# Clustered attention with a spectral gate on one core: routing turned by VectorE, alternating score banks, another last inverse, dummy matmuls in front

## The chip, the cores and the metric

One core of a Trainium2 chip. The metric is the time of one execution on the device in microseconds; the kernel before takes 423.12 us (median of three runs, 422.86 to 423.76). TensorE (PE in the profile) multiplies matrices into PSUM, which has eight banks of 512 fp32 a partition here; VectorE (DVE), ScalarE (ACT) and GpSimd (POOL) work on tiles; SyncE (SP) only issues DMAs. Each engine runs its own instruction stream in order.

## The reference, cut to what matters

```python
# q, k, v: (4, 8, 768, 64); centroids: (8, 16, 64)
q_assign = argmax(einsum('bhsd,hcd->bhsc', q_n, c_n), -1)   # q_n, k_n, c_n: rows scaled to length 1
k_assign = argmax(einsum('bhsd,hcd->bhsc', k_n, c_n), -1)
mask = q_assign[:, :, :, None] == k_assign[:, :, None, :]
scores = where(mask, scale * q @ k^T, -1e9)
attn = softmax(scores) @ v
x = attn with the heads side by side                         # (4, 768, 512)
x1, x2, x3 = split(x @ w_proj, 3)
x2_conv = irfft(rfft(x2) * rfft(filter_fft))                 # over the 768 positions
out = (x1 * x2_conv * x3) @ w_out
```

## The kernel before

**A planner writes the order.** The body calls `op(engine, duration, function, reads, writes, due, ...)` for each small piece of work. `Plan.run` (line 175) then simulates the engines with these durations and emits the pieces in the order of that simulation: of the pieces that are ready it takes, for each engine, the one with the lowest score, which is its due time plus `WAIT` times the wait until it could start, less `SAME` where TensorE stays in the same array mode (line 212). A due time is lowered to what the successors need (line 180). Where a piece names two engines, the one that would end first gets it. `step(i)` (line 375) is the due time of attention step `i`; `SPANS` (line 27) gives those of the four hyenas. The result is a fixed program; the chip only follows it.

**Attention.** The 32 heads go in 16 pairs, two heads on the two halves of the partitions. For each pair:

- `load_pair` (line 389) loads q, k and v from HBM on SP's queue; loads of later pairs stand behind the masks of pair 0 (`masks0`).
- `routing` (line 593) turns q and k by fp32 transposes on TensorE (line 606), copies them to `qkT`, casts them on GpSimd into the operands `aug` (line 613), multiplies by the normed centroids into 4 x 32 rows of a bank, one strip of 32 rows for each of q and k and each half of the sequence (line 623, `sim`), copies that to SBUF (line 626), turns it on TensorE with three fp32 transposes so that the 16 clusters lie along the free axis (line 631), finds the first maximum with five VectorE operations (lines 636 to 642), turns the one-hot back with six bf16 transposes on TensorE into 64 rows by 768 (line 650), scales and shifts it by `mk` on its way out of PSUM (lines 655 and 657: q's rows become 0 or -262144, k's rows 0 or 1), and puts it into 16 extra rows of `aug` with four small DMAs (line 664). With those rows in the operands, a score of two different clusters comes out far below zero.
- `attend` (line 673), six times: scores of 128 keys against 768 queries of both heads into three banks (line 685), one exponential over 1536 columns into `pb` (line 689), its product with v accumulated in two banks (line 699), and a running sum of `pb` on VectorE (line 709).
- `finish` (line 715): sums over the keys, their reciprocals by way of DRAM, the scaled result `rb`, the sum and difference of its halves `uT`, and a bf16 copy `xT`.

**PSUM.** `BankPool.choices` (line 92) says which banks a piece may take: scores always banks 0 to 2, the attention output 3 and 4, all else 5 to 7, and more where attention hasn't begun or no scores are left.

**Hyena.** After each four pairs (one batch), `hyena` (line 775) does the projections, the transform as products with sine and cosine tables `fw`, the product with the filter's spectrum (lines 804 and 807), the inverse transform with `inv`, and the output product. The inverse of a block of 128 channels (line 844) splits into an even part `pe` and an odd part `po`; ScalarE or VectorE copies `po` to `od` (line 858), VectorE forms sum and difference `yy` (line 860), and line 863 multiplies by `x13`, the product of the two gates.

**In front.** `constants`, `centroid` (norms of the centroids), `angles` (line 454: 15 VectorE operations, then six sine activations on ScalarE with a table of their own, line 496), `inverse_tables` (line 508: `inv` by transposing `fw`) and `filter_tables` (line 536: the filter's spectrum, scaled on VectorE into `hm`) prepare tables while pairs 0 and 1 begin.

## Time and profile before

| | |
|---|---|
| median of the runs | 423.12 us |
| the profiled execution: its time, its span | 422.92 us, 421.1 us |
| first and last scores' exponential begin | 21.87 us, 343.51 us |
| last attention product begins | 347.16 us |
| mean granted TensorE clock | 0.984 |
| SP's queue: raw loads, masks, stores | 64, 62, 24 issues |

The span runs from the first to the last instruction. A row of the timeline gives the start in us, the duration in us, engine, line, operation, output and input tiles, how many instructions were merged, and in brackets how long the engine had been idle and what released it. A row of the groups gives the number of instructions, total busy us, mean ns, and the idle time ahead of them. Matmuls overlap in a pipeline, so the distance from start to start says more than a duration. In a table of stretches each engine's busy us is followed by its count of instructions, and then come the granted clock of TensorE, the share of the DMA engines and GB/s.

### The profile page before, as it was taken

How to read it: one execution, taken by the hardware profiler on the slowest of the kernel's cores; microseconds unless marked ns; L12 is line 12 of the kernel's file. 1: busy time of each engine (PE TensorE's matmuls, PEld its weight loads, DVE VectorE, ACT ScalarE, POOL GpSimd, SP SyncE). 2: the span in 40 equal slices, each digit the busy share in tenths (PEclk: the TensorE clock that was granted, in tenths of full speed). 3: DMA queues.
4: the chain of work that ended last, by engine and by line, in shares of the span. 5: the costliest groups of instructions: out<-in, count | busy, mean ns of one | idle time of the engine just before them, and what ended most of it. 6: DMA issues, size and time to landing. Idle time of an engine off the chain costs nothing. (4 is left out here: it accounts for less than half of the span.)

```text
span 421.1 us, 8711 instructions
## 1 busy us (share of the span) xinstructions
PE 393.9 (94%) x3485; PEld 213.6 (51%) x3485; DVE 354.4 (84%) x414; ACT 256.5 (61%) x317; POOL 120.9 (29%) x114
## 2 busy tenths in 40 slices
PE   4489998999999999999999999999999999998794
PEld 2245444445445565655454545545655467555442
DVE  5959977898989898989879799999899788947673
ACT  2477655888577767555775766666676654344242
POOL 5722333155253140532405051407113002101000
PEclk9869999999999999999999999999999999999998
DMA  8199956544363314020365711110311002200123
GB/s 183 20 226 216 222 128 148 129 99 93 87 158 86 84 45 115 10 77 3 76 161 161 164 40 48 48 40 4 84 41 40 3 10 81 101 2 2 75 76 149
DMA packets 68943, 37.17 MB, mean 88 GB/s; under 512 B 56940, under 2 KB 62632, under 8 KB 68904
## 3 DMA queue, kind: packets, MB, share of 16 engines
q1 hardware_dynamic: 67640, 34.45, 31.9%
q0 software_dynamic: 1056, 2.10, 2.7%
q8 instruction: 27, 0.44, 0.4%
q10 hardware_dynamic: 208, 0.08, 0.1%
q14 instruction: 12, 0.10, 0.1%
HBM read 30.66 MB, written 6.48 MB: 88 GB/s over the span
## 5 line engine op out<-in xcount | busy, mean ns | idle before, releaser
L689 ACT ACTIVATE pb<-scores 128x1536 f32<-128x1536 f32 x96 | 139.4, 1452 | 52.2 <-PE scores L324 50.9
L699 PE MATMUL outs<-pb,vraw 128*64 128x512 f32 (+1 forms) x768 | 143.2, 492 | 0.2 <-ACT osb L719 0.2
L313 POOL CAST aug<-qkT 64x768 bf16<-64x768 f32 x64 | 85.1, 1329 | 160.6 <-PE scores L324 80.3
L709 DVE TENSOR_TENSOR acc<-acc,pb 128x1536 f32<-128x1536 f32 x64 | 118.1, 1845 | 9.5 <-ACT pb L689 9.1
L699 PEld LDWEIGHTS outs<-pb,vraw 128*64 128x64 f32 x768 | 54.4, 137 | 66.2 <-issue 59.7
L324 PE MATMUL scores<-aug,aug 128*64 128x512 bf16 (+3 forms) x768 | 81.8, 332 | 5.1 <-DMA aug<-ohT 2.8
L324 PEld LDWEIGHTS <-aug 80*64 80x64 bf16 (+1 forms) x768 | 42.1, 111 | 35.0 <-issue 15.5
L324 PEld LDWEIGHTS <-wpj 128*64 128x64 bf16 x512 | 32.3, 110 | 16.6 <-issue 5.6
L324 PE MATMUL bank<-xT,wpj 128*64 128x384 bf16 x384 | 38.5, 326 | 0.0
L709 DVE TENSOR_TENSOR acc<-pb,pb 128x1536 f32<-128x1536 f32 x16 | 31.8, 1987 | 4.7 <-ACT pb L689 4.7
L606 PE MATMUL bank<-ident,raw 128*128 128x128 f32 x183 | 30.5, 294 | 5.5 <-DMA raw<-in_q_dram 5.4
L324 PEld LDWEIGHTS <-k 128*64 128x64 bf16 (+1 forms) x448 | 21.7, 108 | 22.3 <-issue 11.4
L863 POOL TENSOR_TENSOR k<-yy,x 128x768 bf16<-128x768 f32 x7 | 16.1, 2302 | 58.6 <-DVE yy L860 54.1
L606 PEld LDWEIGHTS bank<-ident,raw 128*128 128x128 f32 x183 | 20.6, 147 | 20.1 <-issue 11.5
L311 ACT COPY qkT<-bank 128x384 f32<-128x384 f32 x47 | 21.8, 482 | 10.3 <-PE bank L606 10.2
L313 POOL CAST xT<-rb 128x768 bf16<-128x768 f32 x8 | 10.6, 1325 | 45.3 <-PE bank L324 20.1
L769 DVE TENSOR_TENSOR uT<-rb 128x384 bf16<-128x384 f32 x32 | 21.4, 680 | 0.1
L324 PE MATMUL bank<-wpj,uT 128*64 128x512 bf16 x160 | 20.6, 380 | 0.0
L804 DVE TENSOR_TENSOR tm<-bank,hm 128x1024 f32<-128x1024 f32 x16 | 19.4, 1219 | 0.8 <-PE bank L533 0.7
L719 ACT COPY osb<-outs 128x769 f32<-128x769 f32 x16 | 12.8, 801 | 8.9 <-PE outs L699 8.9
L764 DVE SCALAR_TENSOR_TENSOR rb<-osb,rb 128x768 f32<-128x768 f32 x16 | 17.8, 1114 | 0.0
L324 PEld LDWEIGHTS <-uT 128*64 128x64 bf16 x192 | 12.6, 109 | 8.6 <-issue 1.9
(161 smaller groups left out, 440.6 us busy)
## 6 DMA issues: line engine op xcount, KB each, us to landing
raw<-in_q_dram SPq DMA_DIRECT2D x32, 192.0 KB
raw<-in_k_dram SPq DMA_DIRECT2D x32, 192.0 KB
vraw<-in_v_dram SPq DMA_DIRECT2D x16, 384.0 KB
rb<-dr SPq DMA_DIRECT2D x30, 192.0 KB
out_dram<-os SPq DMA_DIRECT2D x21, 256.0 KB
k<-in_moe_filter_fft_dram SPq DMA_DIRECT2D x4, 384.0 KB
wpj<-in_moe_w_proj_dram POOLq DMA_DIRECT2D x1, 1536.0 KB, 14.3
aug<-ohT SPq DMA_DIRECT2D x62, 24.0 KB
```

What stands on the lines that cost most here:

```text
L311: nc.scalar.copy(o, i)
L313: eng[e].tensor_copy(o, i)
L324: nc.tensor.matmul(out[64 * c:64 * c + 64], lhsT[:, 64 * c:64 * c + 64], rhs, **k)
L606: nc.tensor.transpose(ps.t[:, ts(t, 128)], rv[:, 3 * ch + t], identp.t)
L689: op("ACT", 1.48, lambda e: nc.scalar.activation(pb.t[:, :, :S], sps.t.rearrange("p (a b) -> p a b", a=2), Act.Exp, scale=0.125), r=[sps], ...
L699: nc.tensor.matmul(o.t[64 * hp:64 * hp + 64, lo:hi], vv.t[:, hp, ts(sk, D)], pb.t[:, hp, lo:hi], start=(sk == 0), stop=(sk == NT - 1))
L709: nc.vector.tensor_tensor(acc.t, a, pb.t[:, :, :S], op=Alu.add)
L719: op("ACT", 0.82, lambda e: nc.scalar.copy(osb.t, o.t[:, :S + 1]), r=[o], w=[osb], due=step(i) + 5.0)
L764: op("DVE", 0.98, lambda e: V.scalar_tensor_tensor(rb.t, osb.t[:, :S], osb.t[:, S:S + 1], rb.t, op0=Alu.add, op1=Alu.mult), r=[osb, rb], w ...
L769: op("DVE", 0.55, lambda e, e_=e_, alu=alu: V.tensor_tensor(uT.t[:, e_], x3()[:, :, :64], x3()[:, :, 64:], op=alu), r=[rb], w=[(uT, e_)], ...
L804: op("DVE", 1.2, lambda e, i=i, cs=cs, ps=ps, tm=tms[cs]: V.tensor_tensor(tm.t, ps.t.unsqueeze(1).to_broadcast([128, 2, DM]), hm.t[:, i, c ...
L863: op(("DVE", "POOL"), (0.95, 1.8), lambda e, dt=dt, yt=yt, x13=x13: eng[e].tensor_tensor(y2v()[:, dt], yt().rearrange("p t c -> p (t c)"), ...
```

## The change

- **Routing.** `sim` is turned by a VectorE transpose of 32 x 32 blocks straight from PSUM; the one-hot goes back by a second such transpose, within SBUF. Both sets of TensorE transposes, the copy of `sim` and two bank takings go. `ohT` is 128 x 384 in place of 64 x 768, `mk` has 128 rows, the scaling works in place, and each of the four mask DMAs becomes two of half the size.
- **Banks.** For the first 24 steps (`TWICE`) scores may take banks 5 to 7 as well as 0 to 2, and other work may take 0 to 2; the three single banks become one tile.
- **Last inverse.** For batch 3 (`DIRECT`), each block's two output halves are full accumulations of six products; the second uses negated tables (`minus`, made on GpSimd). A VectorE product with `x13` follows each straight from PSUM. `od`, `yy` and the sum and difference go there.
- **Front.** `warm` adds 8 and 6 pairs of matmuls on the identity whose results nobody reads. Twelve operations of the angles and the two sums of the filter may go to GpSimd, the scalings of the filter to ScalarE.
- **Planner.** Each group of pieces gets an offset to its due time (`NUDGE`, some 500 numbers from -170 to 313), `SAME` goes from 1.08 to 1.777 and `WAIT` from 82.17 to 148.96. `ADDED` is empty, so its branch in `attend` isn't taken.

```diff
-SAME, WAIT, ANGLES = 1.08, 82.17, 0.99
+DIRECT = (3,)
+ADDED = ()
+TWICE = 24
+SAME, WAIT, ANGLES = 1.777, 148.96, 0.99
+NUDGE = {
+    "const": -26.79, "cent": -40.87, "l0.0": -65.51, "l0.1": -29.45, "v0": -3.48, "l1.0": -122.7,
...
+        o.due += NUDGE.get(o.tag, 0.0)
...
         if k == "S":
-            return [(0, 1, 2)]
+            return [(0, 1, 2)] + ([(5, 6, 7)] if b.scores_begun < b.twice else [])
...
-        if not b.scores_left:
+        if not b.scores_left or 0 < b.scores_begun < b.twice:
             ok += [0, 1, 2]
...
+    def warm(at, n, due):
+
+        P.tag = f"warm{at:.0f}"
+        for _ in range(n):
+            ps = Val(psE)
+
+            def f(e, ps=ps):
+                halves(ps.t, identb.t, identb.t.unsqueeze(1).to_broadcast([128, 4, 128]), start=True, stop=True)
+            op("PE", 0.43, f, r=[identb], w=[ps], due=due, after=at, mode="C64", kind="warm")
...
+            both = (("DVE", "POOL"), (0.36, 0.6))
+            op(*both, lambda e, m=m, n=n: eng[e].tensor_scalar(n(), kc(), st.t[:, m:m + 1], None, op0=Alu.mult),
+               r=[(na, "k"), st], w=[(na, m)], due=due, shared=True)
...
+        op("POOL", 2.0, lambda e: nc.gpsimd.tensor_scalar(
+            minus.t[:, :2], inv.t[:, 2:4], -1.0, None, op0=Alu.mult), r=[inv], w=[(minus, 0)], due=step(60), shared=True)
...
-        op("DVE", 1.76, lambda e: nc.vector.tensor_tensor(fu(), lo.t, hi.t, op=Alu.add),
+        op(("DVE", "POOL"), (1.76, 3.3), lambda e: eng[e].tensor_tensor(fu(), lo.t, hi.t, op=Alu.add),
...
+        both = (("ACT", "DVE"), (0.59, 0.68))
...
-        op(("ACT", "DVE"), (0.486, 0.55), lambda e: copy(e, sim.t, ps.t[:, :384]), r=[ps], w=[sim], due=due)
...
-                nc.tensor.transpose(sT.t[:, ts(t, 128)], sim.t[:, ts(t, 128)], identp.t)
-        op("PE", 0.33, f, r=[sim, identp], w=[sT], takes=[mx, cand], due=due, mode="A")
+        op("DVE", 0.56, lambda e: nc.vector.transpose(sim.t, ps.t[:, :384]), r=[ps], w=[sim], due=due, kind="T1")
...
-                nc.tensor.transpose(tp[:64, t * 128:(t + 1) * 128], ov[:, t % 3, t // 3], identb.t)
-        op("PE", 0.35, f, r=[oh, identb], w=[oT], takes=[ohT], due=due, mode="C64")
+        op("DVE", 0.55, lambda e: V.transpose(ohT.t, oh.t.rearrange("p n c -> p (n c)")), r=[oh], w=[ohT], due=due,
+           kind="T2")
...
-        op(("DVE", "ACT"), (0.68, 0.815), f, r=[oT, mk], w=[ohT], due=due)
+        op(("DVE", "ACT"), (0.22, 0.48), f, r=[mk, ohT], w=[ohT], due=due)
...
+                for ch in range(2):
+                    def f(e, j=j, hp=hp, ch=ch):
+                        r0 = 64 * ch + 32 * j + 16 * hp
+                        eng[e].dma_start(aug.t[hp][j][64 - 16 * hp:80 - 16 * hp, ts(ch, 384)], ohT.t[r0:r0 + 16])
...
+            if b in DIRECT:
+                for e_ in range(2):
+                    ps = Val(psF)
+
+                    def f(e, dt=dt, ps=ps, e_=e_):
+                        for n in range(6):
+                            w = minus.t[:, n - 2] if e_ and n > 1 else inv.t[:, n]
+                            halves(ps.t[:, :384], yv()[:, n // 2, n % 2, ts(dt, 128)], w, start=(n == 0), stop=(n == 5))
+                    op("PE", 0.98, f, r=[y, inv] + [minus] * e_, w=[ps], takes=[y2], due=due, mode="C64", kind="I")
+                    op("DVE", 0.55, lambda e, dt=dt, ps=ps, e_=e_, x13=x13: V.tensor_tensor(
+                        y2v()[:, dt].rearrange("p (t a c) -> p t a c", a=2, c=64)[:, :, e_],
+                        ps.t[:, :384].rearrange("p (t c) -> p t c", c=64),
+                        x13.t.rearrange("p a b -> p (a b)").rearrange("p (t a c) -> p t a c", a=2, c=64)[:, :, e_],
+                        op=Alu.mult), r=[ps, x13], w=[(y2, (dt, e_))], due=due + 1)
...
+    warm(0.0, 8, FIRST - 300.0)
     routing(0)
+    warm(14.0, 6, T0 - 4.0)
```

More of the change, by code (lines that the diff above doesn't have):

```diff
@@ L134 @@
     __slots__ = ("alts", "fn", "deps", "succ", "need", "due", "vals", "takes", "mode", "lag", "size",
-                 "end", "n", "shared", "ready", "kind", "after", "left", "table")
+                 "end", "n", "shared", "ready", "kind", "after", "left", "table", "tag")
 class Plan:
@@ L509, in inverse_tables @@
         for j in range(6):
+            P.tag = f"inv{j}"
             ps = Val(psF)
@@ L705, in attend @@
             acc, last = accs[p], pbs[i - 1]
+            P.tag = f"acc{p}"
             def f(e):
```

188 lines of the change are left out of this document (107 added, 81 removed), and 69 rows, old and new, of the table NUDGE.

## The prediction

> **What bounds the kernel now.** I read the shares of the page first, then the busy time of five stretches cut where the picture changes, then the timeline of both ends.
>
> ```profile
> span 421.1 us, 8711 instructions
> PE 393.9 (94%) x3485; PEld 213.6 (51%) x3485; DVE 354.4 (84%) x414; ACT 256.5 (61%) x317; POOL 120.9 (29%) x114
> ```
> ```profile
> core 0: us, PE busy (x) PEld busy (x) DVE busy (x) ACT busy (x) POOL busy (x), PEclk, DMA share, GB/s
> 0.00:17.00 17.00, 9.12 (x51) 5.28 (x51) 11.85 (x31) 5.60 (x11) 12.22 (x31) 1.00 0.54 118
> 17.00:32.10 15.10, 10.28 (x66) 5.83 (x65) 9.71 (x20) 10.63 (x13) 5.05 (x15) 0.66 0.84 176
> 32.10:348.60 316.50, 314.15 (x2738) 165.43 (x2738) 283.48 (x301) 212.30 (x240) 97.86 (x68) 1.00 0.36 88
> 348.60:380.00 31.40, 30.25 (x322) 19.50 (x319) 23.24 (x35) 13.58 (x25) 3.94 (x2) 1.00 0.14 52
> 380.00:421.10 41.10, 30.11 (x320) 17.61 (x314) 26.14 (x31) 14.40 (x30) 1.81 (x1) 0.96 0.20 77
> ```
>
> The reader should see three regimes. From 32.1 to 348.6 us TensorE idles 2.35 us of 316.5 at full clock: here time is what TensorE is given to do, and VectorE (283.5, 90%) is second. Before 32.1 it is idle 12.7 us and runs at a granted 0.66 from 17 on: a chain of dependencies. After 380 it idles 11.0 us of 41.1 while no engine is full: the hyena of the last batch, a chain again. Each part of the change belongs to one regime.
>
> **Middle: the transposes leave TensorE.** Routing of a pair loses three fp32 transposes of the similarities (line 631) and six bf16 ones of the one-hot (line 650). Mean durations overlap in a pipeline, so I take start to next start.
>
> ```profile
> 100.86 0.50 PE L650 MATMUL bank<-identb,oh 128*64 128x128 bf16 x6
> 101.29 0.55 PE L631 MATMUL bank<-ident,sim 128*128 128x128 f32 x3
> 101.67 0.49 PE L606 MATMUL bank<-ident,raw 128*128 128x128 f32 x3
> ```
> ```profile
> 151.67 0.55 PE L631 MATMUL bank<-ident,sim 128*128 128x128 f32 x3
> 152.15 0.84 PE L324 MATMUL scores<-aug,aug 80*64 80x512 bf16 x8
> ```
> ```profile
> L631 PE MATMUL bank<-ident,sim 128*128 128x128 f32 x45 | 8.2, 291 | 0.0
> ```
>
> The six cost 101.29 - 100.86 = 0.43 us, the three 101.67 - 101.29 = 0.38 beside other transposes and 152.15 - 151.67 = 0.48 where scores follow; entering that mode alone I put at that same difference, 0.10, and half the pairs pay it. That is 0.38 to 0.48 plus 0.43, and 0.05: 0.86 a pair. 45 instructions on this bank kind and 3 on another are 16 pairs; pairs 0 and 1 lie before 32.1, so 14 x 0.86 = **12.0 us**, bounds 14 x 0.71 = 9.9 (six transposes at 0.33, as when they interleave with the next matmul) and 14 x 1.01 = 14.1. All of it counts, since TensorE waits for almost nothing there.
>
> VectorE pays. Nearest rows:
>
> ```profile
> L752 DVE STREAM_TRANSPOSE acc<-scores 128x768 f32<-128x768 f32 x1 | 1.0, 983 | 1.4 <-PE scores L324 1.4
> L637 DVE TENSOR_TENSOR cand<-bank,mx 128x384 bf16<-128x384 f32 x15 | 8.3, 551 | 0.2
> L642 DVE TENSOR_TENSOR oh<-cand,m 128x384 bf16<-128x384 bf16 x16 | 11.5, 721 | 0.3
> L642 DVE TENSOR_TENSOR oh<-cand,m x16: 551/558/1212, 15.9 to 288.6; 128x384 bf16<-128x384 bf16 x16
> L657 DVE TENSOR_SCALAR ohT<-bank,mk 64x768 bf16<-64x768 bf16 x8 | 5.3, 667 | 2.9 <-PE bank L650 2.8
> L313 POOL CAST aug<-qkT 64x768 bf16<-64x768 f32 x64 | 85.1, 1329 | 160.6 <-PE scores L324 80.3 <-ACT qkT L311 36.5 <-ACT sim L311 16.1
> L580 DVE TENSOR_SCALAR hm<-hm 128x512 bf16<-128x512 bf16 x3 | 0.9, 292 | 0.0
> L313 DVE COPY qkT<-bank 128x384 f32<-128x384 f32 x14 | 7.4, 552 | 6.3 <-PE bank L606 5.6 <-POOL aug L313 0.7
> ```
>
> A block transpose of half the width of line 752 lies between half of 983 ns and a copy of 384 (552); I take 0.55 for each of the two, 0.29 to 0.55 for the bf16 one. The first compare now reads its scores from SBUF, so it moves from the 551 ns of line 637 towards line 642, whose inputs both lie in SBUF: 11.5 / 16 = 0.72, +0.17. The scaling shrinks from 0.67 (half the pairs) to at most the 0.29 of line 580. Per pair 0.55 + 0.55 + 0.17 + 0.29 - 0.33 = 1.23, times 14 = 17.2 us: VectorE would hold 283.5 + 17.2 = 300.7 in a stretch of 316.5 - 12.0 = 304.5, 99%, were nothing moved. But line 313's copies (7.4), the scaled rows of the filter and both its sums may go to ScalarE or GpSimd by the new alternatives, and ScalarE has 104 us free. With 7.4 of copies and about half of the new scalings gone it is near 290, 95%. So some of TensorE's gain will be lost to VectorE's queue: I take **+1.5 us**, bounds 0 and +5. Line 642's second row (shortest, median and longest execution) shows where the 0.17 comes from: most take the 0.55 of line 637, a few up to 1.21.
>
> The Trainium skill (SBUF — State Buffer, section Who interferes with whom) says that a VectorE instruction with two SBUF inputs contends with a GpSimd one that reads SBUF, and that one holds the ports for its whole instruction. The casts of line 313 read SBUF, so by that rule each moved compare could wait out a cast of 1.33 us, 14 x 1.33 = 18.6 more on VectorE and the sum that of the first rival below; by the rows it is 0.17 on average and the sum stays.
>
> The masks now leave in eight pieces instead of four.
>
> ```profile
> L664 SPq DMA_DIRECT2D aug<-ohT x62: 512/582/1642, 18.1 to 295.5; - x62
> ```
>
> Four more issues at 0.58 are 2.3 us of SP's queue per pair; behind them stand the loads of later pairs and the four hops of the denominators. Nothing in the middle waits on a mask today, and a mask has most of a pair's 20 us in hand, so I cost them at nothing; without that cover each pair's first scores would come 2.3 us late, 14 x 2.3 = 32 us.
>
> **Front.** The chain to the first exponential and from it to the fourth:
>
> ```profile
> 5.40 1.51 PE L606 MATMUL bank<-ident,raw 128*128 128x128 f32 x6 [5.40 <-DMA raw<-in_q_dram]
> 11.25 0.96 PE L606 MATMUL bank<-ident,raw 128*128 128x128 f32 x6
> 11.35 0.48 ACT L311 COPY sim<-scores 128x384 f32<-128x384 f32 x1 [2.17 <-PE scores L623]
> 13.43 0.54 DVE L636 TENSOR_REDUCE mx<-scores 128x24 f32<-128x384 f32 x1
> 15.88 0.56 DVE L642 TENSOR_TENSOR oh<-cand,m 128x384 bf16<-128x384 bf16 x1
> 18.07 1.51 SPq L664 DMA_DIRECT2D aug<-ohT  x2
> 20.34 1.49 PE L324 MATMUL scores<-aug,aug 80*64 80x512 bf16 x8 [2.85 <-DMA aug<-ohT]
> 21.87 1.45 ACT L689 ACTIVATE pb<-scores 128x1536 f32<-128x1536 f32 x1 [1.24 <-PE scores L324]
> 23.34 1.28 ACT L496 ACT_TABLE_LOAD   x1
> 28.81 1.45 ACT L689 ACTIVATE pb<-scores 128x1536 f32<-128x1536 f32 x1
> 33.02 1.45 ACT L689 ACTIVATE pb<-scores 128x1536 f32<-128x1536 f32 x1
> 35.59 1.46 ACT L689 ACTIVATE pb<-scores 128x1536 f32<-128x1536 f32 x1 [1.12 <-PE scores L324]
> ```
>
> The same six transposes take 1.51 us cold and 0.96 warm; the clock column says 1.00 there, so I go by durations. The first row is q of pair 0; its k I take alike. Fourteen dummy pairs of matmuls cover the idle TensorE before 5.4 and around 14 to 18. Worth: two sets of six, 2 x 0.55 = 1.1; the first scores, cold in the row at 20.34, shrink by the same third, 0.5, and the similarity matmuls before 11.35 I estimate at as much again: 1.0. The turn: from 11.35 to 13.43 is 2.08, becomes one transpose of 0.55 and a gap of 0.1: -1.4. From the end of the one-hot (16.44) to the masks (18.07) is 1.6, becomes 0.55 + 0.3: -0.8. Two more issues on each of the two queues: +1.2. Sum -1.1 - 1.0 - 1.4 - 0.8 + 1.2 = -3.1 to the first exponential. Then 28.81 - 23.32 = 5.5 us go to the sine tables on ScalarE, and the third exponential comes another 4.2 later, because the scores wait for a single bank set and TensorE, at 0.66, is behind. With two sets the second and third scores stand ready and exponentials follow at 1.45: 2.7 less. In TensorE's terms: the 10.3 us busy between 17 and 32.1 are about 6 at full clock and start some 3.1 earlier. I take **-6.5 us**, bounds -3.1 (the chain alone, the sine block stays the wall) and -9.5. That the angles may go to GpSimd I count in these bounds.
>
> **Tail.**
>
> ```profile
> 408.92 1.29 PE L324 MATMUL bank<-inv,k 128*64 128x384 bf16 x16
> 410.14 0.84 PE L324 MATMUL scores<-wout,k 128*64 128x512 bf16 x6
> 410.30 0.48 ACT L311 COPY od<-bank 128x384 f32<-128x384 f32 x1 [0.35 <-PE bank L324]
> 410.86 1.01 DVE L860 TENSOR_TENSOR acc<-bank,od 128x384 f32<-128x384 f32 x2
> 411.91 0.96 DVE L863 TENSOR_TENSOR k<-acc,x 128x768 bf16<-128x768 f32 x1
> ```
>
> Per block of the last inverse one ScalarE copy (0.48), two sums (1.01) and a product (0.96) become two products of 0.55 straight from PSUM: VectorE 4 x (1.97 - 1.10) = 3.5 us less. TensorE does 12 pairs of 384 columns, 0.16 each by 16 matmuls in 1.22, so 1.92 for 1.22: 4 x 0.7 = 2.8 more. The block's chain, 408.92 to 412.87 = 3.95, becomes 1.92 + 0.26 + 0.55 = 2.7. TensorE's 11 us of idleness there can take the 2.8; about half of 4 x 1.2 is on the path: **-2.5 us**, bounds +3 (TensorE's extra counts whole) and -6.
>
> The negated tables are a few GpSimd operations with 70% of that engine free: nothing; without the cover they would delay only line 863's readers. Every due time also gets an offset, so the order is redrawn everywhere. No row prices that: in the middle it can win at most the 2.35 idle, and I put it at 0, bounds ±3.
>
> **Sum.** This profiled execution took 422.92 us, 1.8 more than its span and 0.2 under the median of the runs (423.12). 422.92 - 12.0 + 1.5 - 6.5 - 2.5 = 403.4, with the 0.2 for the median 403.6; I say **403.5**. The bounds that belong together (10 and 14 in the middle, 3.1 and 9.5 in front, +3 and -6 behind) seldom all fall one way; as a spread they give 396 to 412.
>
> **Rivals.**
> VectorE becomes the bound: slower. Its 33 us of idleness in the middle are waits inside an ordered queue; if they stay and 17 us come on top, the stretch is 300.7 + 33 = 333.7 in place of 316.5, and 422.92 + 17.2 - 6.5 - 2.5 is 431. For it: 99% with nothing moved. Against: TensorE hardly waits for VectorE now, so those waits are VectorE's slack. It decides once VectorE is above some 97% there with TensorE waiting on it. 6%.
>
> The front gives only its bound: the sine block stays between the first exponentials. 403.5 + 3.4, and 2.5 of a tail that gains nothing: 409.4. 20%.
>
> The new order also closes half of both ends' idleness, (12.7 + 11.0) / 2 = 11.9 us, of which some 4 are counted above: a further 8 off, 395.5. For it: no engine is full there. Against: nothing in the diff but the offsets does it. 20%.
>
> The split masks hold the first scores of most pairs back, so the change takes nothing off the middle: half of the 32 us back, 419.5. 4%.
>
> **How the numbers follow.** My forecast has 50%. The range, 391 to 415, takes in the second and third rival and leaves the first and last outside. Under 0.2% (0.85 us; the three runs differ by 0.9) is what a measurement here cannot tell from nothing. All cases but the first rival are faster, 0.94; of it 0.02 goes to the last rival reaching the old time: faster 0.92, same 0.02, slower 0.06.
>
> **What would show it.** Lines 631 and 650 gone and TensorE's busy time some 10 lower; two transposes of 384 columns a pair on VectorE near 0.55 us; VectorE at 93 to 97% between the front and the last scores, with TensorE still idle under 2%; the first exponential at about 18.5 and the fourth near 28.5 instead of 35.59; the granted clock at 1.00 from 20 us on; products from PSUM straight behind the last inverse. A first exponential before 19 with the fourth after 33, or a middle in which TensorE waits for VectorE, would make it wrong.

## The result, and the profile after

The changed kernel takes **480.68 us** (median of 4 runs, 479.21 to 487.21) against 423.44 us for the kernel before beside it: a ratio of 1.134, 95% interval 1.129 to 1.139; the run at 487.21 us was in a slower state of the chip and is left out of the ratio. 403.5 us was predicted, with a range to 415. The prediction was wrong in size and in sign.

The page of the changed kernel, span and busy time:

```profile
span 477.1 us, 8612 instructions
PE 401.6 (84%) x3401; PEld 213.8 (45%) x3401; DVE 348.0 (73%) x412; ACT 250.9 (53%) x316; POOL 139.6 (29%) x131
```

TensorE executes 84 instructions less and yet is busy 7.7 us longer, and its idle time went from 27.2 to 75.5 us. VectorE and ScalarE work about as long as before (348.0 for 354.4 us, 250.9 for 256.5), and GpSimd, 18.7 us busier, is still only 29% busy. No engine is fuller; every engine waits.

To see where, I cut both executions at the first exponential of pair 1 and at the last exponential. The table of stretches of the kernel before, then of the changed one (busy us of TensorE, its weight loads, VectorE, ScalarE, GpSimd; granted clock; DMA share; GB/s):

```profile
43.41:343.51 300.10, 297.75 (x2597) 156.22 (x2599) 267.15 (x286) 200.43 (x227) 94.30 (x63) 1.00 0.33 83
343.51:421.10 77.59, 65.44 (x676) 40.20 (x672) 54.48 (x69) 30.74 (x57) 7.03 (x4) 0.98 0.18 67
```
```profile
17.00:32.10 15.10, 6.63 (x34) 4.08 (x34) 9.91 (x15) 9.32 (x13) 8.08 (x11) 0.59 0.88 175
...
60.72:402.03 341.31, 300.21 (x2541) 155.44 (x2539) 271.78 (x296) 200.15 (x232) 103.73 (x70) 1.00 0.27 68
402.03:477.10 75.07, 62.77 (x620) 38.38 (x616) 42.10 (x56) 24.03 (x45) 7.23 (x4) 0.95 0.16 60
```

The front grew by 17.3 us (43.41 to 60.72), the middle by 41.2 (300.1 to 341.3), the tail shrank by 2.5. In the middle TensorE now idles 341.31 - 300.21 = 41.1 us, where it idled 2.35. What its waits look like, from the timeline of the changed kernel:

```profile
160.13 1.49 PE L400 MATMUL rest<-xT,wpj 128*64 128x384 bf16 x16
...
161.66 0.48 ACT L949 COPY x<-rest 128x384 f32<-128x384 f32 x1 [0.50 <-PE rest L400]
...
162.19 0.85 PE L738 MATMUL rest<-qkT,cbd 128*32 128x384 f32 x8 [0.57 <-ACT x L949]
...
163.11 0.48 ACT L949 COPY x<-rest 128x384 f32<-128x384 f32 x1 [0.97 <-PE rest L738]
163.64 0.84 PE L400 MATMUL rest<-k,fw 128*64 128x512 bf16 x6 [0.60 <-ACT x L949]
```

TensorE writes `rest`, ScalarE copies `x` out of it, TensorE waits for that copy and only then writes `rest` again. Before, these rows had `bank` as their tile. There are three banks behind either name, so a write to one should not have to wait for a copy from another; here they take turns. `rest` is the single tile of 1536 columns that the change makes of three single banks, in a line that my prediction read as a gain only.

### The profile page after: what moved, and what is told of

Read it like the earlier page. It is cut to its first block, busy times and chain, and to the rows that moved or that the text cites. A ratio compares the mean times of both kernels' runs of the same rounds, so it can differ in the third digit from the quotient of the medians.

```text
span 477.1 us, 8612 instructions
## 1 busy us (share of the span) xinstructions
PE 401.6 (84%) x3401; PEld 213.8 (45%) x3401; DVE 348.0 (73%) x412; ACT 250.9 (53%) x316; POOL 139.6 (29%) x131
## 3 DMA queue, kind: packets, MB, share of 16 engines
q1 hardware_dynamic: 69624, 34.46, 28.5%
## 5 line engine op out<-in xcount | busy, mean ns | idle before, releaser
L796 ACT ACTIVATE pb<-scores 128x1536 f32<-128x1536 f32 x88 | 127.8, 1453 | 46.4 <-PE scores L400 44.9
L400 PE MATMUL scores<-aug,aug 80*64 80x512 bf16 (+1 forms) x704 | 74.7, 330 | 8.0 <-ACT pb L796 4.2
L400 PE MATMUL rest<-xT,wpj 128*64 128x384 bf16 x384 | 38.8, 331 | 12.7 <-DVE tm L922 4.1
L387 ACT COPY qkT<-rest 128x384 f32<-128x384 f32 x47 | 21.3, 482 | 25.9 <-PE rest L719 10.6
L922 DVE TENSOR_TENSOR tm<-rest,hm 128x1024 f32<-128x1024 f32 x20 | 24.1, 1221 | 14.5 <-PE rest L400 7.2
L719 PE MATMUL rest<-ident,raw 128*128 128x128 f32 x156 | 26.0, 291 | 9.2 <-ACT qkT L387 4.2
L389 POOL CAST xT<-rb 128x768 bf16<-128x768 f32 x12 | 15.9, 1325 | 60.4 <-DVE rb L880 48.8
L719 PEld LDWEIGHTS rest<-ident,raw 128*128 128x128 f32 x156 | 16.9, 144 | 24.9 <-issue 7.5
L400 PE MATMUL rest<-wpj,uT 128*64 128x512 bf16 x160 | 20.1, 381 | 6.4 <-ACT k L387 6.1
L949 ACT COPY x<-rest 128x384 f32<-128x384 f32 x24 | 11.3, 481 | 22.1 <-PE rest L400 15.7
```

The lines of the kernel that those rows point to most:

```text
L387: nc.scalar.copy(o, i)
L389: eng[e].tensor_copy(o, i)
L400: nc.tensor.matmul(out[64 * c:64 * c + 64], lhsT[:, 64 * c:64 * c + 64], rhs, **k)
L719: nc.tensor.transpose(ps.t[:, ts(t, 128)], rv[:, 3 * ch + t], identp.t)
L796: op("ACT", 1.48, lambda e: nc.scalar.activation(pb.t[:, :, :S], sps.t.rearrange("p (a b) -> p a b", a=2), Act.Exp, scale=0.125), r=[sps], ...
L922: op("DVE", 1.2, lambda e, i=i, cs=cs, ps=ps, tm=tms[cs]: V.tensor_tensor(tm.t, ps.t.unsqueeze(1).to_broadcast([128, 2, DM]), hm.t[:, i, c ...
```

## Experiments: the three banks in one tile

**before_onetile.** The kernel before, its order untouched; only the declaration is that of the change:

```diff
-                  [psum.tile([128, 512], F32, name=f"bank{i}") for i in range(3)])
+                  psum.tile([128, 1536], F32, name="rest"))
```

> The kernel before, its order of work unchanged (the planner's own end is 417.6 us with and without the edit), only banks 5 to 7 made views of one tile as in the changed kernel. If work on different banks of one tile is made to wait for each other: far slower, 450 to 490 us, with TensorE waiting on ScalarE's and VectorE's reads of another bank. If the new order of work, or VectorE's queue, is the cause of the loss: 423 us, no change.

Measured: 484.92 us, ratio 1.140 (1.133 to 1.147). Its middle, in the table of stretches:

```profile
50.97:399.53 348.56, 309.23 (x2597) 160.35 (x2599) 267.13 (x286) 201.07 (x227) 90.88 (x63) 1.00 0.27 67
```

The same 2597 instructions take 348.56 us in place of 300.10. One declaration, with no instruction more or less, makes the old kernel as slow as the changed one. TensorE's waits from 60 to 345 us (in all, how often, the longest), the longest row of the kernel before, then the first rows of before_onetile:

```profile
PE bank L650 <- DVE oh L642: 1.3, 1, 1.3
```
```profile
PE rest L323 <- DVE tm L803: 3.6, 5, 1.1
PE rest L323 <- DVE x L832: 1.6, 2, 0.9
PE rest L323 <- ACT x L829: 1.5, 2, 1.2
PE rest L323 <- ACT k L310: 1.4, 2, 0.7
```

TensorE idles 33.1 us of this stretch with one tile and 2.05 us before, in many short waits of a write to `rest` for a reader of `rest`. The profile infers them from semaphores, so they are waits in the program; which part of the tools puts them there, no run shows.

**after_ownbanks.** The other way round: the changed kernel in its own order, with three tiles of one bank again. Where scores take these three, their exponential comes in three pieces of 512 columns.

```diff
-                  psum.tile([128, 1536], F32, name="rest"))
+                  [psum.tile([128, 512], F32, name=f"bank{i}") for i in range(3)])
...
-        op("ACT", 1.48, lambda e: nc.scalar.activation(
-            pb.t[:, :, :S], sps.t.rearrange("p (a b) -> p a b", a=2), Act.Exp, scale=0.125),
+            for to, x in ((pb.t[:, 0, :512], sps.t[0]), (mid, sps.t[1].rearrange("p (a b) -> p a b", a=2)),
+                          (pb.t[:, 1, 256:S], sps.t[2])):
+                nc.scalar.activation(to, x, Act.Exp, scale=0.125)
```

> The changed kernel with its order unchanged (planner's end 411.2 us in both), but banks 5 to 7 are three tiles again; exponentials of scores that lie there are done in three pieces of 512 columns (12 of 96 steps or so, about 0.3 us more each). If the one tile is the cause: 410 to 422 us, faster than before. If the offsets' order or VectorE's queue is the cause: 470 to 485 us.

Measured: 432.93 us, ratio 1.019 (1.013 to 1.025). That is outside both expected ranges and much nearer the first. The one tile is worth 480.68 - 432.93 = 47.8 us. What remains is still 8 to 9 us above the kernel before, and 29 above the forecast. The rest of the runs is about that.

The spans of all profiled executions used below, cut at the same exponentials (their starts in ScalarE's timeline):

| kernel | first exponential | first of pair 1 | middle (to the last exponential) | tail (to the end) | time, median us |
|---|---|---|---|---|---|
| before | 21.87 | 43.41 | 300.1 | 77.6 | 423.4 to 424.4 |
| after | 24.61 | 60.72 | 341.3 | 75.1 | 480.68 |
| after_ownbanks | 23.97 | 58.44 | 302.4 | 68.5 | 432.93 |
| own_latew | 24.21 | 49.82 | 304.1 | 68.6 | 425.02 |
| before_turn | 22.07 | 57.47 | 294.2 | 77.7 | 431.68 |
| turn_nowire | 21.93 | 43.12 | 308.9 | 77.6 | 429.25 |
| turn_sameorder | 24.25 | 46.47 | 307.8 | 77.6 | 432.33 |
| turn_maskpool | 23.82 | 45.64 | 298.0 | 77.7 | 423.74 |
| turn_nodve | 22.38 | 44.58 | 293.5 | 77.7 | 417.46 |
| turn_dvepad | 23.02 | 45.27 | 296.5 | 77.7 | 420.99 |

## Experiments: the front of the new order

**own_latew.** after_ownbanks loses its front between pair 0 and pair 1. Its order stays; only the two large weight loads on GpSimd's queue are issued later, just before pair 4's casts.

```diff
     def emit(self, o, e):
+        if o.tag == "w":
+            self.held.append((o, e))
+            return
+        if o.tag == "cast4":
+            while self.held:
+                x, y = self.held.pop(0)
+                x.fn(y)
         o.fn(e)
```

> The kernel after with its own bank tiles again (432.93 us), its order unchanged but for one thing: the two large weight loads on POOL's queue (wpj and wout, 2 MB as moved, issued at 34.16 and 35.16 us there) are issued only just before the fifth pair's casts, near 61 us. Theory that they starve the raw loads: TensorE's wait of 7.79 us for a raw k load ends, the first exponential of pair 1 (58.44 us there) comes 6 to 10 us earlier, and the time falls to 423 to 427 us. Rival, that the raw loads are late because SP issues them late (SP waits at the eight mask pieces and for free raw buffers): no change beyond 2 us, 431 to 433 us.

Measured: 425.02 us, ratio 1.003 (1.000 to 1.005). TensorE's wait in after_ownbanks, with SP's queue around it:

```profile
38.89 5.09 SPq L461 DMA_DIRECT2D raw<-in_q_dram  x2
44.08 7.16 SPq L461 DMA_DIRECT2D raw<-in_k_dram  x2
```
```profile
49.83 0.87 PE L719 MATMUL scores<-ident,raw 128*128 128x128 f32 x3 [7.79 <-DMA raw<-in_k_dram]
```

And SP's queue and the first exponential of pair 1 in own_latew:

```profile
38.19 2.80 SPq L470 DMA_DIRECT2D raw<-in_k_dram  x2
```
```profile
49.82 1.46 ACT L811 ACTIVATE pb<-scores 128x1536 f32<-128x1536 f32 x1 [0.46 <-PE scores L409]
```

The new order puts transposes of a later pair's raw k ahead of pair 0's last scores, and so of pair 1's first, in TensorE's queue. With 2 MB of weights on their way, that k is issued at 44.08 and held up; without them the same two loads leave at 38.19, and pair 1 begins 8.6 us earlier. 7.9 us of the loss are this. Pair 1 still begins 6.4 us after the kernel before.

**own_nowarm.** after_ownbanks without the dummy matmuls (`if o.kind != "warm": o.fn(e)`).

> The kernel after with its own bank tiles again (432.93 us), order unchanged, without the dummy matmuls at the front. My prediction's reading, that they bring the granted clock up early and so the first scores: the stretch of 17 to 32 us gets a clock below the 0.50 to 0.64 it has with them and the first exponential (23.97 us) comes 1 to 3 us later, 434 to 436 us. Rival, that the clock falls again in the wait before the first scores whatever ran before it: first exponential and time unchanged within 1 us. A second rival, that the dummy matmuls delay the real transposes in front of them: 0.5 to 1 us faster.

Measured: 434.31 us, ratio 1.025 (1.021 to 1.028); the first exponential comes at 25.00 instead of 23.97, and the granted clock from 17 to 24 us is 0.50 instead of 0.64, from 24 to 32 it is 0.50 in both. The dummies bring 1 us at the first exponential. In the time, 1.4 us more with overlapping intervals, they can't be told from nothing.

## Experiments: the routing edit by itself

**before_turn.** The kernel before with the routing edit (both VectorE transposes, eight mask pieces) and nothing else; the planner draws its order anew.

```diff
-        op(("ACT", "DVE"), (0.486, 0.55), lambda e: copy(e, sim.t, ps.t[:, :384]), r=[ps], w=[sim], due=due)
+        op("DVE", 0.56, lambda e: nc.vector.transpose(sim.t, ps.t[:, :384]), r=[ps], w=[sim], due=due, kind="T1")
...
-        op("PE", 0.35, f, r=[oh, identb], w=[oT], takes=[ohT], due=due, mode="C64")
+        op("DVE", 0.55, lambda e: V.transpose(ohT.t, oh.t.rearrange("p n c -> p (n c)")), r=[oh], w=[ohT], due=due,
+           kind="T2")
```

> The kernel before with only the routing's edit (both block transposes on VectorE, masks in eight pieces), three separate bank tiles, no offsets. The planner draws a new order for it with an end of 426.4 us against 417.6 for the kernel before. If taking the transposes off TensorE pays as in the prediction: 411 to 414 us. If VectorE's queue or the split masks take over: 425 to 440 us. The one tile plays no part here.

Measured: 431.68 us, ratio 1.017 (1.010 to 1.024). The middle is 5.9 us shorter, but pair 1 begins at 57.47.

**turn_nowire.** The same, but the planner no longer queues the mask pieces behind the weight loads in its own model (`size=12288` becomes `size=0`).

> The kernel before with the routing edit alone (431.68 us), but the planner takes the eight mask pieces of a pair to land 2 us after their issue instead of putting them behind the large weight loads in its model of the transfers; in the profile of that kernel the first pieces of pair 1 were issued at 29.64 and 32.27 us and yet its first exponential came at 57.47 us. If the order alone delays pair 1 (TensorE's queue was laid out for masks that the planner put at 53 us): first exponential of pair 1 near 43 to 46 us, time 418 to 423 us. If the pieces really land late behind the large loads: the first exponential of pair 1 stays past 53 us and the time at 429 to 433 us.

Measured: 429.25 us, ratio 1.012 (1.007 to 1.017). Pair 1 begins at 43.12, so before_turn's late front was its order and no late data. But the time hardly moved: the middle is 14.7 us longer than in before_turn. Part of this is where the cut falls: before_turn has 60 matmuls fewer behind the first exponential of pair 1 (2414 against 2474) and TensorE 11.1 us less busy there, so much of its late front was filled with work of the middle. Part may be the execution, since the profiled one of turn_nowire took 431.40 us, 2 us over the median. Two redrawn orders of one edit can't be compared stage by stage to the size of the edit, so the following runs keep the order of the kernel before on every engine.

**turn_sameorder and before_mask8.** In turn_sameorder VectorE's transposes stand where the copy and TensorE's second transposes stood, nothing stands where the first ones stood, and two mask pieces stand where one transfer stood. before_mask8 has the old routing, with each mask transfer cut in two:

```diff
-                    eng[e].dma_start(aug.t[hp][j][64 - 16 * hp:80 - 16 * hp], ohT.t[r0:r0 + 16])
+                    for ch in range(2):
+                        eng[e].dma_start(aug.t[hp][j][64 - 16 * hp:80 - 16 * hp, ts(ch, 384)], ohT.t[r0:r0 + 16, ts(ch, 384)])
```

> The kernel before with the routing edit alone, and the order of every engine as it was before: where the first turn's copy stood, VectorE's block transpose; nothing where TensorE's first transposes stood; VectorE's second block transpose where TensorE's second ones stood; two mask pieces where one transfer stood. My prediction's steps 2 to 4 without a new order: TensorE some 10 us less busy, and of it about 8 to 10 us gained, 413 to 416 us. Rival, that VectorE's added work (two transposes of 0.55 us a pair and copies that ScalarE made) makes other things late by as much as TensorE is relieved: 421 to 426 us, with new waits of TensorE on VectorE of 5 us and more in the stretch of 60 to 340 us. A second rival, that the routing edit loses by itself: near 431 us, as with its new order.

> The kernel before with its order, each of the four mask transfers of a pair cut in two halves of 384 columns: eight issues on SP instead of four, nothing else. My prediction's step 4 costs this at nothing: 423 to 424 us. Rival, that the added issues on SP's queue push the denominators' round trip and the raw loads behind them, for which VectorE and TensorE wait in order: 425 to 428 us, with more waiting of VectorE on the denominators' return than the 5.9 us in three waits of before.

Measured: 432.33 us, ratio 1.019 (1.017 to 1.022), and 432.39 us, ratio 1.018 (1.015 to 1.021). Cutting the masks costs 8.4 us with nothing else changed, and the routing edit costs the same as its masks alone. So the second rival of turn_sameorder, 431 us, comes out in the time, and before_mask8 gives the reason: the edit loses through the masks. The price of the cut itself, 8.4 us, is above both ranges expected for before_mask8.

**own_maskpool, turn_maskpool and before_maskpool.** If SP's queue is what the pieces cost, another queue gives it back. In own_latew, turn_sameorder and the kernel before, the masks of pair 1 and later are issued on GpSimd's queue, at the same places:

```diff
-                        eng[e].dma_start(aug.t[hp][j]
+                        (nc.gpsimd if p else eng[e]).dma_start(aug.t[hp][j]
```

> The kernel after with its own bank tiles and late weight loads (425.02 us), the mask pieces of pair 1 and later issued on POOL's queue instead of SP's, at the same places of the order. If SP's queue is what makes the denominators' return late (9.5 us of VectorE's waiting in four waits in that kernel): 419 to 423 us and less of that waiting. Rival, that SP has room and POOL's casts of the next pair now wait behind its eight issues: 425 to 432 us.

> The kernel of the routing edit in the old order (432.33 us), with the eight mask pieces of pair 1 and later issued on POOL's queue at the same places of the order; pair 0's stay where they are. Cutting the masks of before in two cost 8.4 us by itself. If that is SP's queue, in which the way back of the denominators stands behind the pieces: some 5 to 8 us come back, 424 to 427 us. If besides the queue had hidden what TensorE was relieved of: down to 414 to 420 us. Rival, that the pieces are late by their number and not by their queue, or that POOL's casts now wait behind them: 430 to 436 us.

> The kernel before (424.0 us) with its four mask transfers of pair 1 and later on POOL's queue instead of SP's, nothing else. If SP's queue already costs in the kernel before (VectorE waits 5.9 us for the denominators there, TensorE 2.35 us in all of the middle): 0 to 2 us faster, since TensorE has almost no idle time to give. Rival, that POOL's casts and gathers then wait behind masks that are not ready: 425 to 430 us.

Measured: own_maskpool 424.68 us, ratio 1.000 (0.998 to 1.003), no change that can be told from own_latew, though 419 to 423 had been expected; turn_maskpool **423.74 us**, 1.000 (0.998 to 1.001), 8.6 us back; before_maskpool **422.91 us**, 0.998 (0.997 to 0.999), 0.2% below the kernel before and the fastest kernel here that computes the reference. In the old order SP's queue was the whole price of the pieces. How it worked, from the timeline of turn_sameorder, SP's queue and then VectorE:

```profile
229.02 3.72 SPq L662 DMA_DIRECT2D aug<-ohT  x6
...
233.41 1.14 SPq L662 DMA_DIRECT2D aug<-ohT  x2
...
236.70 0.58 SPq L735 DMA_DIRECT2D dr<-dn  x1
...
241.19 0.50 SPq L738 DMA_DIRECT2D rb<-dr  x1
```
```profile
227.36 0.23 DVE L734 RECIPROCAL dn<-dn 128x12 f32<-128x12 f32 x1 [1.80 <-DMA dn<-dd]
...
247.16 1.02 DVE L762 SCALAR_TENSOR_TENSOR rb<-osb,rb 128x768 f32<-128x768 f32 x1 [3.98 <-DMA rb<-dr]
```

and what TensorE waited for behind that:

```profile
251.98 1.05 PE L324 MATMUL bank<-wpj,uT 128*64 128x512 bf16 x8 [1.86 <-DVE sim L627]
...
259.45 0.55 PE L607 MATMUL bank<-ident,raw 128*128 128x128 f32 x3 [1.61 <-DVE k L313]
...
261.24 1.51 PE L726 MATMUL bank<-acc,ones 128*32 128x384 f32 x8 [1.24 <-DVE acc L707]
```

The same place in the kernel before, SP's queue and VectorE:

```profile
219.27 1.81 SPq L664 DMA_DIRECT2D aug<-ohT  x3
...
221.75 0.96 SPq L664 DMA_DIRECT2D aug<-ohT  x1
...
224.86 0.58 SPq L737 DMA_DIRECT2D dr<-dn  x1
```
```profile
218.97 0.22 DVE L736 RECIPROCAL dn<-dn 128x12 f32<-128x12 f32 x1
```

And in turn_maskpool, SP's queue, VectorE, GpSimd's next pieces:

```profile
225.28 1.41 SPq L735 DMA_DIRECT2D dr<-dn  x1
...
230.60 0.49 SPq L738 DMA_DIRECT2D rb<-dr  x1
```
```profile
221.93 0.22 DVE L734 RECIPROCAL dn<-dn 128x12 f32<-128x12 f32 x1
...
237.62 0.97 DVE L762 SCALAR_TENSOR_TENSOR rb<-osb,rb 128x768 f32<-128x768 f32 x1
```
```profile
239.52 3.83 POOL L662 DMA_DIRECT2D aug<-ohT  x8
```

The denominators go to DRAM and back in four hops on SP's queue. With the pieces on it, the reciprocal is done at 227.59 and its hop `dr<-dn` leaves at 236.70, 9.1 us later: six and two pieces, 4.9 us of issuing, stand between them. In the kernel before it is 5.7 us (219.19 to 224.86), with four transfers between, and with the pieces on GpSimd 3.1 us (222.15 to 225.28). Behind it the last hop, `rb<-dr`, leaves at 241.19, and VectorE, which is in order, stands 3.98 us at `rb`; in turn_maskpool it does not wait there at all. The work behind `rb` in VectorE's queue (the turn of the next similarities, a copy, a running sum) is what TensorE then waits for. No mask was late for its own reader here; the masks made something else late.

## Experiments: what TensorE's relief is worth

turn_maskpool is the routing edit with the price of its masks taken away in the middle, and it gains nothing. TensorE is busy 383.9 us there against 393.9 before, the 10 us that the prediction named as a sign.

**turn_nodve, turn_dvepad and before_dvepad.** turn_nodve is turn_maskpool without VectorE's two transposes (the scores are copied unturned, the one-hot is scaled as it is). turn_dvepad puts two transposes back at the same places, into tiles that nothing reads. before_dvepad adds such transposes to before_maskpool, where TensorE still makes its own.

```diff
-        op(("ACT", "DVE"), (0.486, 0.55), lambda e: nc.vector.transpose(sim.t, ps.t[:, :384]), r=[ps], w=[sim], due=due)
+        op(("ACT", "DVE"), (0.486, 0.55), lambda e: copy(e, sim.t, ps.t[:, :384]), r=[ps], w=[sim], due=due)
...
-            nc.vector.transpose(ohT.t, oh.t.rearrange("p n c -> p (n c)"))
+            pass
...
+            nc.vector.transpose(pad2, oh.t.rearrange("p n c -> p (n c)"))
```

(the last line stands in the two padded kernels only; their other added transpose reads the similarities in PSUM, in turn_dvepad only where ScalarE makes the copy, so that VectorE's count there is that of turn_maskpool)

> The kernel of the routing edit in the old order with its masks on POOL's queue (423.74 us), with both of VectorE's block transposes left out too: the first turn is the plain copy that before had, the second is nothing, and the scaling reads the one-hot rows as they are. (So the scores are not turned and the routing comes out different; the mask pieces, the sizes and the order are the same.) TensorE is then relieved of its transposes and VectorE not loaded with them. If VectorE's added work of 11.4 us ate TensorE's relief of 10.0 us: 413 to 418 us. If TensorE's relief is lost for another reason (waits on transfers, or a chain that neither engine sets): 421 to 424 us.

> The kernel without VectorE's block transposes (417.46 us; the scores are not turned there and the routing comes out different), with two block transposes a pair put back on VectorE at the same places, into tiles that nothing reads: VectorE is loaded as in the turned kernel (423.74 us), but the chain from the similarities to the masks does not run through them. If the 6.3 us between the two kernels are VectorE's load: 422 to 425 us. If they are the longer chain of dependent steps to the masks: 416 to 419 us.

> The kernel before with its masks on POOL's queue (422.91 us) and two block transposes a pair added on VectorE, where the turned kernel has them, whose results nothing reads: some 18 us of VectorE's work more (16 pairs, two of 0.57 us), TensorE's own transposes stay. My prediction's step 3 would have at most 5 us for such work, since it took VectorE's idle time of 3 to 8% in the middle to cover it: 423 to 428 us. If VectorE is as much the bound of the middle as TensorE: 431 to 441 us.

Measured: turn_nodve 417.46 us, ratio 0.984 (0.982 to 0.986); turn_dvepad 420.99 us, 0.994 (0.992 to 0.995); before_dvepad 427.60 us, 1.009 (1.006 to 1.012). The middle in the tables of stretches of turn_maskpool and of turn_nodve:

```profile
45.64:343.64 298.00, 289.39 (x2480) 146.20 (x2480) 277.49 (x313) 192.12 (x214) 143.98 (x175) 1.00 0.35 84
```
```profile
44.58:338.05 293.47, 287.66 (x2480) 144.22 (x2481) 268.62 (x287) 197.77 (x226) 145.91 (x175) 1.00 0.35 85
```

With 8.9 us less on VectorE (277.49 to 268.62) and the same matmuls on TensorE, the middle is 4.5 us shorter and pair 1 begins 1.1 us earlier. So taking the transposes off TensorE, with the steps and bank writes that go with them, is worth 6.3 us here (5.5 against before_maskpool), and VectorE's transposes take all of it back. Loading VectorE without touching the chain (turn_dvepad) brings 3.5 of these 6.3 us back. I put the other 2.75 down to the two transposes being steps of the chain from similarities to masks; no run shows that by itself. Neither theory's range held turn_dvepad, and ScalarE still makes the plain copies there that the transposes replace in turn_maskpool. VectorE was 267.15 of 300.10 busy before, 89%, and 277.49 of 298.00, 93%, after: its work was no longer free. It doesn't hold TensorE directly, though: of TensorE's 8.6 us of idleness in the middle of turn_maskpool 6.8 are waits for ScalarE, mostly for exponentials, and 1.5 for VectorE. By which path VectorE's work reaches the exponentials, I have not followed.

**turn_act.** turn_maskpool with VectorE's copies of `qkT` and its scalings made by ScalarE.

```diff
-                op(("ACT", "DVE"), (0.486, 0.55), lambda e, j=j, ch=ch, ps=ps: copy(e, qkT[j].t[:, ch], ps.t[:, :384]),
+                op(("ACT", "DVE"), (0.486, 0.55), lambda e, j=j, ch=ch, ps=ps: copy("ACT", qkT[j].t[:, ch], ps.t[:, :384]),
```

> The kernel of the routing edit in the old order with its masks on POOL's queue (423.74 us), with VectorE's 14 copies of the turned queries and keys (0.55 us each) and its 8 scalings (0.38 us) made by ScalarE instead, at the same places: some 10.7 us less on VectorE, some 12 us more on ScalarE (53 to 60% busy). If VectorE's load is what TensorE's relief went into: 416 to 421 us. If ScalarE's exponentials, for which TensorE waits in that kernel (5.3 us in ten waits), become later by it: 423 to 428 us.

Measured: 429.31 us, ratio 1.012 (1.009 to 1.015), outside both ranges. The loss is in front: pair 1 begins at 50.98, since the moved work stands between the sine activations there and the second exponential comes at 34.60 in place of 30.77. The middle is 298.8 us against 298.0: VectorE's load went down by 7.7 us in all, 5.6 of them in the middle, and nothing of it came to TensorE, which waits there 7.4 us for ScalarE. That would fit a ScalarE as much in the way as VectorE, but this run moved both loads at once and can't tell.

**own_nodirect.** after_ownbanks with `DIRECT = ()`: the old last inverse, with the order up to there and the offsets kept.

> The kernel after with its own bank tiles again (432.93 us), without the full-depth last inverse; the list of due-time offsets stays, and with it the order up to the last inverse. The tail from the last exponential to the end was 77.6 us before and is 68.5 us with both. If the full-depth inverse brings it, it goes back to some 76 us and the time to 440 us; if the offsets bring it by another order of the tail, the tail stays at 69 to 70 us and the time at 433 to 435 us.

Measured: 434.34 us, ratio 1.025 (1.021 to 1.029). The tails, with the full-depth inverse and without it:

```profile
360.81:429.30 68.49, 59.37 (x620) 38.61 (x616) 41.38 (x55) 23.75 (x45) 7.25 (x4) 0.99 0.18 66
```
```profile
363.68:435.80 72.12, 59.98 (x588) 35.01 (x584) 44.62 (x58) 25.69 (x49) 9.05 (x5) 0.95 0.17 63
```

Of the 9.1 us by which the tail of after_ownbanks is shorter than the old one (77.6), 3.6 go with the full-depth inverse at most: the profiled execution of own_nodirect, 437.91 us, is its longest, 3.6 us over the median, with a granted clock of 0.95 in the tail against 0.99. In the times the difference is 1.4 us and the intervals overlap. The 5.5 us that stay are not all won. The new order puts 88 matmuls, 48 of them projections, ahead of the last exponential that used to stand behind it (588 in the tail here, 676 before), so TensorE is busy 60.0 us in this tail instead of 65.4 and idle 12.1 us as before. What left the tail is paid in the middle.

## Why the prediction was wrong

**The step that failed: the banks.** The part on the front counted only that scores may take two sets of banks; that "the three single banks become one tile", as the description of the change has it, got no term of the sum, no bounds and no rival. It costs 48 us in the new order (after_ownbanks) and some 60 in the old one (before_onetile). Without it the prediction would still have failed, in sign too, by the steps below.

**The masks at nothing.** "Nothing in the middle waits on a mask today" was right and the wrong question. The text named the four hops of the denominators behind the masks on SP's queue, and didn't ask who waits for them. The price without cover was worked out as late first scores (32 us); what came, in the old order, was 8.4 us; one place of turn_sameorder shows it as VectorE waiting for a hop.

**"All of it counts, since TensorE waits for almost nothing there."** The relief came out smaller than the term: 10.0 us less busy over all 16 pairs of turn_maskpool, 0.63 a pair where 0.86 was taken, and 8.4 in the middle where 12.0 were forecast and 9.9 was the bound. What failed above all is that it counts. In turn_nodve the middle shrinks by 6.6 of it; with VectorE's transposes, by 2.1. A TensorE that is 99% busy says how much work it had, not that the others would keep up with a faster one.

**VectorE pays +1.5.** Undersized: 6.3 us of time for two transposes a pair. Their duration was predicted (567 and 574 ns against 0.55 us; the bf16 one gains nothing from its width), and so was the dearer compare: 720 ns forecast, 716 in the old order (turn_maskpool), 631 in the changed kernel. From the groups of VectorE, the compare of turn_maskpool, then rows of the changed kernel:

```profile
L637 DVE TENSOR_TENSOR cand<-sim,mx 128x384 bf16<-128x384 f32 x16 | 11.5, 716 | 0.2
```
```profile
L748 DVE TENSOR_TENSOR cand<-sim,mx 128x384 bf16<-128x384 f32 x16 | 10.1, 631 | 0.3
L755 DVE STREAM_TRANSPOSE ohT<-oh 128x384 bf16<-128x384 bf16 x16 | 8.9, 567 | 0.3
L741 DVE STREAM_TRANSPOSE sim<-rest 128x384 f32<-128x384 f32 x13 | 7.5, 574 | 10.9 <-PE rest L400 3.6 <-ACT inv L387 2.8 <-PE rest L843 2.3
L762 DVE TENSOR_SCALAR ohT<-ohT,mk 128x384 bf16<-128x384 bf16 x4 | 2.8, 704 | 0.1
```

The scaling on VectorE was forecast at 0.29 us at most and took 0.70 on average here, 0.38 in turn_maskpool. As a bound of 0 to +5 us the term was right for a TensorE that has all its old work (before_dvepad: +4.7 us) and wrong for one that has less.

The means of the compare hide two kinds. In turn_maskpool four of the 16 took 1.17 or 1.18 us and the rest 0.54 to 0.61; in the changed kernel two took 1.17 and 1.21, the rest 0.49 to 0.60. Each long one has a GpSimd cast running over it, but so have some of the short ones. In the kernel before, where the compare reads its scores from a PSUM bank, all 16 took 0.54 to 0.56 us, seven of them under a cast. The scaling of the changed kernel shows the same: two at 0.38, two at 1.03 under casts.

The Trainium skill (SBUF — State Buffer, section Who interferes with whom) has a VectorE instruction with two SBUF inputs contend with a GpSimd one that reads SBUF. The traces agree in kind. The price is some 0.6 us for a few of the compares, 0.17 us on average as the rows had it, and not the 1.33 us of a whole cast each time: the 18.6 us worked out from that did not come.

**The front, -6.5.** The chain to the scores was only half as good: the first half of them starts at 18.02 us where 20.34 - 3.1 = 17.2 was meant, but the second half waits for a GpSimd cast until 19.83, and they end at 20.68 where they had ended at 21.83. The exponential behind them came later still, since the new order put the sine activations ahead of it. ScalarE and TensorE of the changed kernel:

```profile
19.14 1.28 ACT L595 ACT_TABLE_LOAD   x1 [5.51 <-POOL aug L515]
20.44 1.35 ACT L595 ACTIVATE fw<-k 128x384 bf16<-128x384 f32 x3
21.69 1.61 ACT L592 ACTIVATE fw<-k,quarter 128x384 bf16<-128x384 f32 x3
23.32 1.28 ACT L796 ACT_TABLE_LOAD   x1
24.61 1.45 ACT L796 ACTIVATE pb<-scores 128x1536 f32<-128x1536 f32 x1
25.96 1.45 ACT L796 ACTIVATE pb<-rest 128x1536 f32<-128x1536 f32 x1
```
```profile
19.83 0.85 PE L400 MATMUL scores<-aug,aug 128*64 128x256 bf16 x4 [1.29 <-POOL aug L389]
...
26.12 1.11 PE L719 MATMUL scores<-ident,raw 128*128 128x128 f32 x4 [4.15 <-ACT pb L796]
```

The first exponential comes at 24.61 instead of 18.5, the second follows at once from the second set of banks as predicted, and then TensorE's next work waits 4.15 us for the first to leave its banks, at a granted clock of 0.59 in this stretch instead of 1.00. The fourth comes at 40.23, where 28.5 was forecast; with own banks at 38.09, still behind the 35.59 of the kernel before. Nor does the turn shorten the chain as worked out (-1.4, -0.8, +1.2): in the old order the first exponential moves from 21.87 to 23.82 with the routing edit (turn_maskpool) and to 22.38 without its transposes (turn_nodve), since VectorE is busy with the angles there and each step of the chain stands in its queue.

**The tail, -2.5, and the offsets at 0.** The tail gained 9 us with own banks, beyond the bound of -6. The inverse itself was sized about right: 1.4 us by the times, 3.6 at most by the profiles. The larger part came with the new order, which moves work from the tail into the middle; I had put the offsets at 0 for the middle's 2.35 us of idleness, and their win at the ends into a rival of 20%.

**The rivals.** VectorE as the bound (431 us) had the right sign and came nearest, at 6%; its mechanism is part of what turn_nodve shows, but 48 of the 57 us are none of it. What should have stood among the rivals, on the slower side, is the one tile.

What stands open: with own banks and late weights the changed kernel is within 0.3% of the old one (425.02 us), made of +6.4 us in front, +4.0 in the middle and -9.0 behind. Since work went from the tail to the middle, the two belong together: 372.7 us against 377.7 before. With the old front in place, such an order would be some 5 us faster than both, by my estimate from these spans; it was not tried.

## What to carry to other kernels

When an edit merges or splits tiles, price it as an edit of waits: ask of each writer which readers of the whole tile it now follows, even where the storage stays the same. When a transfer is cut in pieces, look for what stands behind it on its queue and who waits for that, not only for who waits for the pieces. And work moved off a full engine counts only as far as the other engines keep up: before moving 10 us onto an engine that is 89% busy, give that load a price of its own. Here two transposes a pair cost 4.7 us where TensorE kept its old work and 6.3 us where it had less.

## What the runs showed that was not expected

- Three PSUM banks in one tile serialize TensorE and its readers: 348.56 us for a middle of 300.10, with identical instructions. TensorE's busy time in it rises too, from 297.75 to 309.23.
- A VectorE block transpose of 128 x 384 takes 567 ns in bf16 and 574 in fp32.
- A VectorE compare of two SBUF inputs took 0.54 to 0.61 us or, in four of 16 cases of turn_maskpool, all under a GpSimd cast, 1.17 or 1.18 us; with its scores in PSUM it never took more than 0.56.
- Eight mask pieces take 5.01 us to issue on SP (turn_sameorder) and 3.83 us on GpSimd (turn_maskpool); four more of them a pair on SP cost 8.4 us a run, and moving the eight to GpSimd's queue brought 8.6 us back.
- The dummy matmuls before 17 us raised the granted clock from 0.50 to 0.64 from 17 to 24 us and left it at 0.50 from 24 to 32 (after_ownbanks against own_nowarm, one profile each).
